# Asking for the expert weights batch by batch, each pair of transfers behind the turned attention weights of its batch

## The chip, the core and the metric

The kernel runs on one core of a Trainium2 chip. The core has engines that work side by side, each with a queue of its own that is worked off in order: TensorE (matrix products; PE in the profile, its weight loads PEld), VectorE (DVE), ScalarE (ACT), GpSimd (POOL) and SyncE (SP, which here only issues transfers). Sixteen transfer engines (DMA) move data between the main memory (HBM) and the core's memory (SBUF); they are fed by a hardware queue, filled from SyncE, and by a software queue, filled from GpSimd. The metric is the device time of one execution in microseconds (us), the median over runs.

## The reference

Two stages. The first is a Nyström attention over 8 batches and 8 heads, 576 positions, 64 values a head; the second sends each of the 4608 tokens through one of 8 experts.

```python
q_lm, k_lm = means of 18 neighbouring rows of q, k      # 32 landmarks a head
A  = softmax(q    @ k_lm.T)                             # 576 x 32
Bm = softmax(q_lm @ k_lm.T)                             # 32 x 32
C  = softmax(q_lm @ k.T)                                # 32 x 576
Z  = Bm.T / (norm1(Bm) * norminf(Bm) + 1e-6)
for _ in range(6): Z = 2 * Z - Z @ Bm @ Z               # inverse by iteration
x = A @ Z @ C @ v                                       # then tokens x 512

e_idx  = argmax(x @ w_gate); gate_w = softmax(x @ w_gate)[e_idx]
eom    = sigmoid(x @ w_output_gate)
out[i] = gate_w * eom[e_idx] * (relu(x[i] @ w1[e_idx]) @ w2[e_idx])
```

An expert has w1 of 512 x 1024 and w2 of 1024 x 512 in float32, 4 MB together, and 8 experts have 33.5 MB.

## The kernel before

The attention runs over the 8 batches, and in each over two halves of four heads; four heads of 32 landmarks fill the 128 partitions. The expert weights of all eight experts have a place of their own, the tile `wall`, which holds them as bfloat16; the transfer itself converts. `load_expert(e)` (L73 to L77) asks GpSimd's software queue for w1 (L74) and w2 (L76) of one expert. In the kernel before it is called at the head of batch `b` for expert `b` (L149). Nothing in the batch reads it.

For each half of a batch:

- SyncE asks for the v tile `vS` in three transfers (L156).
- `turned` (L112 to L132) is called for q and then for k. SyncE asks for the tile `nat` as it lies in memory (L116; two slots). VectorE turns it to `tr` (L118; three slots). GpSimd adds 18 rows to the landmark sums in five steps (L120 to L125, `t9` with one slot, result `lm`). VectorE turns `lm` to `lmT` (L127), and GpSimd builds the block-diagonal matrix `bd` from it (L130, twice, four slots).
- TensorE makes the landmark scores `pB` (L165), the scores of C and of A (both by the helper `scores`, L144), each from a `bd` and a `tr`.
- VectorE, ScalarE and GpSimd make the softmaxes. The last part of it, for A: VectorE turns the scores to `At` (L210) and takes the maximum `ax` (L212), GpSimd subtracts (L216), ScalarE exponentiates (L217), VectorE sums (L218), GpSimd multiplies (L220), and VectorE turns the result to `AT` (L222; four slots). `ATs[1]` is that of the second half.

After both halves, the inverse is iterated for both together (L230 on TensorE, L234 to L241 on VectorE, each step waiting for the one before), GpSimd spreads the result to `ZB` (L246), TensorE makes the gate logits `pL` (L267) and the rows `pX` (L276), ScalarE converts them to `xo` (L279), and SyncE stores them to `x_rows` in main memory (L280).

When all batches are done, the routing sorts the tokens by expert (L282 to L457). Then 43 tiles of 128 tokens go through the experts: GpSimd gathers rows of `x_rows` (L469), TensorE multiplies by the weights in `wall` (L488, L506) at an offset that is read from the sorted list, and GpSimd scatters the result (L511).

The order of each engine's queue is not written out by hand. A planner lays out all instructions when the kernel is built: it takes them in the order of the program as their priority, with its own model of when inputs and tile slots come free, and so mixes work of several batches. On the chip each queue then keeps that order. Semaphores are added so that an instruction waits for what it reads and overwrites; a waiting instruction holds up all behind it on its engine.

Of the kernel before, what the change touches and what calls it, by code (L numbers as in the profile page):

```python
# [36 lines left out]
def kernel(  # L37
# [11 lines left out]
    nc = tc.nc  # L49
# [12 lines left out]
    W1 = DCH * F  # L62
# [7 lines left out]
    gp = ctx.enter_context(tc.tile_pool(name="const", bufs=1))  # L70
    wall = gp.tile([128, E, WE], BF16)

    def load_expert(e):  # L73
        nc.gpsimd.dma_start(out=wall[:, e, :W1].rearrange("p (c f) -> p c f", f=F),  # L74
                            in_=moe_w1[e].rearrange("(c p) f -> p c f", p=128))
        nc.gpsimd.dma_start(out=wall[:, e, W1:].rearrange("p (c d) -> p c d", d=HD),  # L76
                            in_=moe_w2[e].rearrange("(c p) d -> p c d", p=128))  # L77
# [14 lines left out]
    with tc.tile_pool(name="attn_c", bufs=1) as cp, \  # L92
# [53 lines left out]
            return p[:, :, :NC]  # L146

        for b in range(B):
            load_expert(b)  # L149
            XW = sb.tile([128, 2, 128 + D], F32, tag="X", bufs=3)  # L150
            cc = sb.tile([128, 2], F32, tag="cc")
            ATs = []
            for hf in range(2):
# [67 lines left out]
                AT = sb.tile([128, S], F32, tag="AT", bufs=4)  # L221
                nc.vector.transpose(out=AT, in_=At.rearrange("p k r -> p (k r)"))  # L222
                ATs.append(AT)


            cur = XW
# [328 lines left out]
```

## Time and profile before

| | |
|---|---|
| median of 3 runs | 617.27 us (615.83 to 618.49) |
| the profiled execution | 616.98 us, its span 615.3 us |
| first and last start of a TensorE matmul on batch data | 27.5 us, 604.7 us |
| last `AT` turned | 327.1 us |
| last store to `x_rows` issued | 370.0 us |
| first gather of the experts' stage | 418.4 us |
| busy in the span | TensorE 465.4 us, GpSimd 286.6, VectorE 277.3, ScalarE 126.3 |
| weight transfers | 16, issued by GpSimd between 1.6 and 60.3 us |

A view of stages gives the busy microseconds of each engine in a stretch with the number of instructions in brackets, then the granted TensorE clock (1.00 is full speed), the mean busy share of the sixteen transfer engines, and the rate in GB/s. The share can exceed 1 where transfers overlap on an engine. A row of a timeline gives the start in us, the length in us, the engine and line, the operation with the tile written and the tiles read, the shape, the count, and in square brackets how long the engine had stood idle and what ended that. SPq marks the issue of a transfer on SyncE. A row of landing times gives the microseconds from the issue of a transfer to its end.

### The profile page before, as it was taken

The numbers are of one execution on the slowest core, as the hardware profiler recorded it, in microseconds if no ns is written. First come the engines' busy times: TensorE is split into PE (matmuls) and PEld (weight loads), VectorE is DVE, ScalarE is ACT, GpSimd is POOL, SyncE is SP. The second block draws the span as 40 slices with busy tenths as digits, with TensorE's granted clock in tenths as the row PEclk, the third lists the DMA queues.
The fourth block names the chain that finished last, engine by engine and source line by source line (L and its number), as shares of the span: only waits on it lengthen the run. The fifth ranks groups of instructions, "written<-read, shape, count | busy, mean of one in ns | idle before, by whom it ended". The sixth has DMA issues, their size and how long they took to land. (4 is left out here: it accounts for less than half of the span.)

```text
span 615.3 us, 9095 instructions
## 1 busy us (share of the span) xinstructions
PE 465.4 (76%) x3094; PEld 290.7 (47%) x3094; DVE 277.3 (45%) x681; ACT 126.3 (21%) x283; POOL 286.6 (47%) x408
## 2 busy tenths in 40 slices
PE   0231776788888788688798783494999999999993
PEld 0121453564666456365564442472555555555551
DVE  0223375374465546545462304991444444444442
ACT  0020121313232131222213120001222222222220
POOL 1754879628465574874712002005445445444321
PEclk9966597797798889898887776556999999999997
DMA  9999999552427053352310000002222222223200
GB/s 162 259 228 242 246 260 264 136 145 73 152 75 205 9 146 116 94 138 78 116 38 27 14 29 11 0 2 68 69 87 101 89 104 86 99 92 99 74 27 0
DMA packets 35948, 65.51 MB, mean 106 GB/s; under 512 B 5088, under 2 KB 24032, under 8 KB 35904
## 3 DMA queue, kind: packets, MB, share of 16 engines
q0 software_dynamic: 18048, 31.86, 22.9%
q1 hardware_dynamic: 17856, 33.07, 17.9%
q8 instruction: 27, 0.44, 0.3%
q14 instruction: 17, 0.14, 0.1%
HBM read 67.53 MB, written 15.99 MB: 136 GB/s over the span
## 5 line engine op out<-in xcount | busy, mean ns | idle before, releaser
L144 PE MATMUL p<-tr,bd 128*128 128x288 f32 x256 | 87.4, 465 | 44.9 <-POOL bd L130 44.1
L488 PE MATMUL ph<-wall,xT 128*128 x344 | 82.9, 385 | 2.3 <-issue 2.3
L511 POOL DMA_INDIRECT out_dram<-ysb,sca_i x43 | 43.5, 1012 | 81.9 <-DVE ysb L510 51.1
L506 PE MATMUL py<-wall,hT 128*128 x344 | 81.1, 379 | 0.0
L144 PEld LDWEIGHTS p<-tr,bd 128*128 128x128 f32 x256 | 51.8, 218 | 55.0 <-POOL bd L130 44.6
L492 ACT ACTIVATE h<-ph 128x512 bf16<-128x512 f32 x86 | 46.7, 594 | 138.4 <-PE ph L488 138.4
L469 POOL DMA_INDIRECT xs<-x_rows,gat_i x43 | 42.0, 976 | 65.7 <-DVE sca_i L456 42.6
L276 PE MATMUL pX<-ZB,AT 128*128 128x256 f32 (+1 forms) x160 | 54.8, 460 | 15.1 <-POOL ZB L246 7.6
L230 PE MATMUL pN<-nxt 128*128 128x192 f32 x192 | 46.6, 367 | 16.7 <-DVE nxt L238 11.9
L500 DVE COPY hT<-pht 128x1024 bf16<-128x1024 bf16 x43 | 29.7, 691 | 62.4 <-PE pht L498 62.4
L118 DVE STREAM_TRANSPOSE tr<-nat 128x1152 f32<-128x1152 f32 x32 | 43.5, 1360 | 25.6 <-DMA nat<-in_q_dram 20.8
L488 PEld LDWEIGHTS <-xT 128*128 128x128 bf16 x344 | 33.9, 99 | 43.9 <-issue 4.4
L120 POOL TENSOR_TENSOR t<-nat 128x576 f32<-128x576 f32 x32 | 44.9, 1404 | 15.7 <-DMA nat<-in_q_dram 14.9
L510 DVE TENSOR_SCALAR ysb<-py,coeff_s 128x512 f32<-128x512 f32 x43 | 32.3, 751 | 40.0 <-PE py L506 40.0
L230 PEld LDWEIGHTS pN<-nxt 128*128 128x128 f32 x192 | 35.0, 208 | 30.3 <-DVE nxt L238 20.3
L506 PEld LDWEIGHTS <-hT 128*128 128x128 bf16 x344 | 31.9, 98 | 30.7
L276 PEld LDWEIGHTS pX<-ZB,AT 128*128 128x128 f32 (+1 forms) x160 | 27.6, 198 | 30.7 <-ACT xo L279 11.3
L130 POOL TENSOR_TENSOR bd<-mask,lmT 128x128 f32<-128x128 f32 x64 | 27.8, 457 | 29.5 <-PE p L144 16.0
L216 POOL TENSOR_TENSOR At<-At,ax 128x576 f32<-128x576 f32 x16 | 18.5, 1157 | 42.3 <-DVE ax L212 42.2
L279 ACT CAST xo<-pX 128x512 bf16<-128x512 f32 (+1 forms) x40 | 23.4, 584 | 33.8 <-PE pX L276 28.5
L428 PE MATMUL pinv<-Vt,St 128*128 128x86 f32 x72 | 22.1, 465 | 8.7 <-DVE Vt L426 8.7
L498 PEld LDWEIGHTS <-h 128*128 128x128 bf16 x344 | 22.9, 98 | 11.1 <-ACT h L492 0.6
(143 smaller groups left out, 619.8 us busy)
## 6 DMA issues: line engine op xcount, KB each, us to landing
wall<-in_moe_w_dram POOLq DMA_DIRECT2D x16, 1024.0 KB, 32.5
vS<-in_v_dram SPq DMA_DIRECT2D x48, 192.0 KB, 3.8
nat<-in_q_dram SPq DMA_DIRECT2D x16, 576.0 KB, 5.3
nat<-in_k_dram SPq DMA_DIRECT2D x16, 576.0 KB, 5.0
x_rows<-xo SPq DMA_DIRECT2D x32, 128.0 KB, 1.7
xs<-x_rows,gat_i POOLq DMA_INDIRECT x43, 2.8
out_dram<-ysb,sca_i POOLq DMA_INDIRECT x43, 2.8
x_rows<-xo SPq DMA_DIRECT2D x8, 64.0 KB, 1.9
```

The source lines that it names most:

```text
L118: nc.vector.transpose(out=tr.rearrange("p k c r -> p (k c r)"), in_=nat.rearrange("p k d -> p (k d)"))
L120: nc.gpsimd.tensor_tensor(t9, nat[:, 0:9], nat[:, 9:18], op=ADD)
L144: nc.tensor.matmul(p[:, n, :NC], lhsT=bd[:, c].rearrange("p h r -> p (h r)"), rhs=rhs, start=(c == 0), stop=(c == 1))
L230: nc.tensor.matmul(pN[:, hf, :], lhsT=cur[:, hf, :128], rhs=cur[:, hf, :])
L276: nc.tensor.matmul(pX[:tk, hf * HH * D:(hf + 1) * HH * D], lhsT=ATs[hf][:, t0:t0 + tk], rhs=ZB[:, hf].rearrange("p h d -> p (h d)"))
L469: nc.gpsimd.indirect_dma_start(out=xs, out_offset=None, in_=x_rows, in_offset=bass.IndirectOffsetOnAxis(ap=gat_i[:, j:j + 1], axis=0))
L488: nc.tensor.matmul(ph[hf], lhsT=xT[:, dc, :], rhs=wf[:, bass.ds(we[j] + (dc * F + hf * 512), 512)], start=(dc == 0), stop=(dc == DCH - 1))
L492: nc.scalar.activation(out=hs[j][:, hf * 512:(hf + 1) * 512], in_=ph[hf], func=RELU)
L500: nc.vector.tensor_copy(hTs[j], pht)
L506: nc.tensor.matmul(py, lhsT=hT[:, fc, :], rhs=wf[:, bass.ds(we[j] + (W1 + fc * HD), HD)], start=(fc == 0), stop=(fc == FCH - 1))
L510: nc.vector.tensor_scalar(out=ysb, in0=py, scalar1=coeff_s[:, j:j + 1], scalar2=None, op0=MUL)
L511: nc.gpsimd.indirect_dma_start(out=out, out_offset=bass.IndirectOffsetOnAxis(ap=sca_i[:, j:j + 1], axis=0), in_=ysb, in_offset=None, bound ...
```

## The change

The call moves from the head of batch `b` to the point behind its second half, in front of the iteration. `load_expert` gets the tile `ATs[1]` as an argument. Before each pair of transfers GpSimd copies one element of that tile into the first element of the two places that the transfers will overwrite. The transfers overwrite what the copies wrote, so they cannot be issued before the copies, and these wait for the tile `AT` of the second half.

```diff
-    def load_expert(e):
+    def load_expert(e, after):
+
+        for c in (0, W1):
+            nc.gpsimd.tensor_copy(wall[:1, e, c:c + 1], after[:1, :1])
         nc.gpsimd.dma_start(out=wall[:, e, :W1].rearrange("p (c f) -> p c f", f=F),
                             in_=moe_w1[e].rearrange("(c p) f -> p c f", p=128))
         nc.gpsimd.dma_start(out=wall[:, e, W1:].rearrange("p (c d) -> p c d", d=HD),
                             in_=moe_w2[e].rearrange("(c p) d -> p c d", p=128))
@@
         for b in range(B):
-            load_expert(b)
             XW = sb.tile([128, 2, 128 + D], F32, tag="X", bufs=3)
@@
                 AT = sb.tile([128, S], F32, tag="AT", bufs=4)
                 nc.vector.transpose(out=AT, in_=At.rearrange("p k r -> p (k r)"))
                 ATs.append(AT)
+            load_expert(b, ATs[1])
 
 
             cur = XW
```

## Prediction

> **What bounds the kernel now.** I read the page first: how busy the engines and the transfer engines are along the span.
>
> ```profile
> span 615.3 us, 9095 instructions
> PE   0231776788888788688798783494999999999993
> DMA  9999999552427053352310000002222222223200
> q0 software_dynamic: 18048, 31.86, 22.9%
> ```
>
> The digits are tenths of a slice of 15.4 us. TensorE has almost nothing to do in the first four slices, while the transfer engines are full in the first seven. After that the roles turn over. The next view gives the stages, in its columns for stage, length, the five engines (PE, PEld, DVE, ACT, POOL), granted clock, transfer share and rate; the last row is from a second call of it.
>
> ```profile
> 0.00:27.50 27.50, 0.00 (x0) 0.00 (x0) 5.35 (x14) 0.00 (x0) 10.43 (x22) 1.00 1.00 211
> 27.50:61.00 33.50, 11.92 (x76) 8.43 (x76) 8.86 (x20) 4.12 (x8) 17.51 (x25) 0.66 1.17 233
> 61.00:101.00 40.00, 26.79 (x143) 18.50 (x143) 20.43 (x44) 5.58 (x13) 33.38 (x56) 0.80 1.15 256
> ...
> 139.00:324.00 185.00, 150.84 (x1125) 103.43 (x1125) 97.73 (x238) 47.88 (x121) 110.86 (x174) 0.89 0.36 103
> ...
> 418.40:615.30 196.90, 180.45 (x1204) 96.78 (x1204) 76.33 (x129) 46.67 (x86) 85.47 (x86) 0.96 0.24 78
> ```
>
> From 139 to 324 us TensorE is busy 150.84 of 185 us, 82%: it bounds that stage, with waits between. In the first 101 us it does 11.92 + 26.79 = 38.7 us of work, which at 82% would take 47 us. So 54 us of the start are lost to something else. What that is stands in SyncE's queue, in the landing times of the natural-order tiles `nat` (first those asked for before 15 us, then the one between 66 and 70 us, the one between 70 and 78, and all after 125 us) and in POOL's order of work.
>
> ```profile
> 5.45 0.44 SPq L116 DMA_DIRECT2D nat<-in_q_dram  x1
> ...
> DMA to landing us min/median/max: 13.0/14.2/15.5
> ...
> DMA to landing us min/median/max: 6.8/6.8/6.8
> ...
> DMA to landing us min/median/max: 6.1/6.1/6.1
> ...
> DMA to landing us min/median/max: 3.5/4.0/6.2
> ```
>
> ```profile
> 18.47 1.41 POOL L120 TENSOR_TENSOR t<-nat 128x576 f32<-128x576 f32 x1 [14.94 <-DMA nat<-in_q_dram]
> 19.82 0.80 POOL L74 DMA_DIRECT2D wall<-in_moe_w_dram  x1
> ...
> 27.01 0.86 POOL L130 TENSOR_TENSOR bd<-mask,lmT 128x128 f32<-128x128 f32 x2 [1.33 <-DVE lmT L127]
> 27.84 1.39 POOL L120 TENSOR_TENSOR t<-nat 128x576 f32<-128x576 f32 x1
> ...
> 37.05 0.92 POOL L76 DMA_DIRECT2D wall<-in_moe_w_dram  x1 [2.70 <-DMA wall<-in_moe_w_dram]
> 39.54 0.86 POOL L130 TENSOR_TENSOR bd<-mask,lmT 128x128 f32<-128x128 f32 x2 [1.58 <-DVE lmT L127]
> ...
> 60.30 0.92 POOL L76 DMA_DIRECT2D wall<-in_moe_w_dram  x1 [3.93 <-DMA wall<-in_moe_w_dram]
> 61.24 0.88 POOL L130 TENSOR_TENSOR bd<-mask,lmT 128x128 f32<-128x128 f32 x2
> ...
> 67.03 0.87 POOL L130 TENSOR_TENSOR bd<-mask,lmT 128x128 f32<-128x128 f32 x2
> ```
>
> The first q tile, asked for at 5.45 us, lands 13.0 us later; with no weights under way the median is 4.0. Then POOL, which adds up the landmarks and builds the block-diagonal `bd`, has the issues of the weight transfers among its additions and twice stands behind a weight transfer (2.70 and 3.93 us). The four `bd` of batch 0 (q and k of each half) are started at 27.01, 39.54, 61.24 and 67.03. TensorE waits for the first and the third:
>
> ```profile
> 61.76 2.29 PE L144 MATMUL p<-tr,bd 128*128 128x288 f32 x4 [12.72 <-POOL bd L130]
> ```
>
> **The change part by part.** The sixteen weight issues leave the head of POOL's queue. Their prices:
>
> ```profile
> L74 POOL DMA_DIRECT2D wall<-in_moe_w_dram x8: 787/792/977, 1.6 to 55.2; - x8
> L76 POOL DMA_DIRECT2D wall<-in_moe_w_dram x8: 914/917/961, 2.6 to 60.3; - x8
> ...
> L488 PE MATMUL ph<-wall,xT x344: 376/379/634, 423.7 to 598.6; 128*128 x172
> ...
> DMA to landing us min/median/max: 8.5/32.5/54.9
> ```
>
> *Step 1, first q tile.* It no longer shares the engines with a pair of weight transfers, but still with the v and k tiles. Bounds: 4.0 us (the quiet median) and 13.0. I take 6.7, an estimate between the 6.1 and the 6.8 that single tiles took while weights still ran, since here three v transfers stand ahead of it on the queue. Gain 6.3 us. It lands at about 12.1.
>
> *Step 2, POOL up to the first `bd`.* Between 18.47 and 27.01 stand five issues, three of L74 and two of L76: 3 x 0.79 + 2 x 0.92 = 4.2 us. Gain so far 10.5, first `bd` at 16.5.
>
> *Step 3, up to the second `bd`.* Between 27.84 and 39.54 stand two L74, three L76 and the wait of 2.70: 1.6 + 2.8 + 2.7 = 7.0 us. Gain so far 17.5.
>
> *Step 4, up to the third `bd`.* Two of each and the wait of 3.93: 1.6 + 1.8 + 3.9 = 7.4 us. Gain so far 24.9 in POOL's present order; the fourth `bd` follows the third as before. That is one end. The other: the planner that orders the queues no longer sees the loads and may put the additions of the second half ahead of the work that waits for VectorE. Then POOL is bound only by its own additions, 4.3 us a tile (27.01 - 18.47 less the 4.2 of issues), so four tiles after 12.1 us end at 29.3 instead of 67.03: gain 37.7. What is late next there is the slot of the transposed tile `tr` (three of them), freed by the scores. I take 30, between the two ends.
>
> *Step 5, the issues come back.* Each batch now has, behind its last turned tile `AT`, two one-element copies and the pair of issues on POOL. The rows for the wait, and for the pace of the batches:
>
> ```profile
> 83.47 1.16 POOL L220 TENSOR_TENSOR At<-At,ax 128x576 f32<-128x576 f32 x1
> ...
> 100.97 1.41 POOL L246 TENSOR_TENSOR ZB<-mask,nxt 128x256 f32<-128x256 f32 x2
> ...
> 109.94 1.16 POOL L220 TENSOR_TENSOR At<-At,ax 128x576 f32<-128x576 f32 x1
> ...
> 140.92 1.16 POOL L220 TENSOR_TENSOR At<-At,ax 128x576 f32<-128x576 f32 x1 [0.58 <-DVE ax L219]
> ...
> 325.90 1.16 POOL L220 TENSOR_TENSOR At<-At,ax 128x576 f32<-128x576 f32 x1 [0.58 <-DVE ax L219]
> ...
> 355.76 1.41 POOL L246 TENSOR_TENSOR ZB<-mask,nxt 128x256 f32<-128x256 f32 x2 [15.54 <-DVE nxt L241]
> ```
>
> ```profile
> L222 DVE STREAM_TRANSPOSE AT<-At x16: 759/778/779, 55.0 to 327.1; 128x576 f32<-128x576 f32 x16
> ```
>
> POOL's own L220 is the input of that transposition, so in the worst order POOL waits its 0.78 us right behind L220. No row shows a one-element copy on POOL; the nearest small ones bound it:
>
> ```profile
> 0.31 0.10 POOL L539 MEMSET const-float32-0.0<- 128x1 f32 x1 [0.31 <-issue]
> ...
> 24.63 0.34 POOL L125 TENSOR_TENSOR lm<-t 128x64 f32<-128x64 f32 x1
> ```
>
> I take 0.2 us each, nearer the single-column row. So a pair costs POOL 0.8 + 0.4 + 1.7 = 2.9 us; seven pairs with work behind them, 20 us. Queued behind them are the additions and `bd` of a later batch, for which TensorE waits. The cover is TensorE's own work: from 139 to 324 us it waited for `bd` once in five batches,
>
> ```profile
> PE p L144 <- POOL bd L130: 3.8, 1, 3.8
> ```
>
> so I take a fifth to a quarter, 5 us. The ends are 0 (the issues are only moved, so a further gain is excluded) and 20 (the cover is gone).
>
> *Step 6, sharing.* The software queue took 22.9% of 615.3 = 141 us of all sixteen engines; the experts' stage used 0.24 x 196.9 = 47 of that at most, so a pair of weights takes about 94 / 8 = 11.7 us. A batch every 37.0 us ((325.90 - 140.92) / 5) uses 0.36 x 37.0 = 13 us without weights, and 25 of 37 with them. The engines do not become the bound. A tile that meets a pair lands in 6.1 to 6.8 us instead of 4.0; I cost that at nothing, because the tiles are asked for ahead of use (two `nat`, three `tr`). Rival 3 is the case without that cover.
>
> *Step 7, the last pair.* It is issued after 327.1 + 0.8 us. With the longest landing, 54.9 us, all is there by 385, against a first use at 423.7; both ends move together. Cost 0. The Trainium skill, in "DMA: Bandwidth & Descriptors", section "Rules for kernel authors", advises the opposite of this change: issue a transfer early and wait for it late. Taken alone it would leave only step 5, 622 us. The 13.0 beside 4.0 us disagrees: early transfers that nobody awaits delayed awaited ones.
>
> Not counted: the granted clock of 0.66 between 27.5 and 61 us, which may rise if TensorE is fed sooner (11.92 us at 0.89 would be about 3 us less).
>
> **Sum.** The profiled execution took 616.98 us, 0.3 below the median of 617.27. 617.0 - 30 + 5 = 592 us.
>
> **The rivals.**
>
> 1. *All of the start is won and the issues stay hidden.* Against it speak the `tr` slots; for it, POOL's 60% load (110.86 of 185). 617 - 37.7 = 579 us.
>
> 2. *The early gain is given back.* The L220 of second halves stand at 83.47, 109.94, 140.92: 26.5 and 31.0 us apart, against 37.0 later. Batches 1 and 2 caught up because the tail of the batch before them came late; if they run at 37.0 at once, 10.5 + 6.0 = 16.5 of the 30 us go. Against it: ZB went from 100.97 with nothing to catch up. 617 - 30 + 16.5 + 5 = 608 us.
>
> 3. *Slower: late `nat` tiles at every batch.* POOL and VectorE start a batch's front with them. If two of the four loads of a batch meet the pair, and each lands up to 2.8 us later on the path (6.8 against 4.0), that is 5.6 us a batch, 39 over seven, against 30 won: 617 - 30 + 39 = 626 us. It decides from 30 / 7 = 4.3 us a batch. For it: the 6.1 and 6.8 us above, taken beside weights. Against: after the start TensorE hardly waits for the front.
>
> 4. *Issues stretched by VectorE.* The pairs now meet a VectorE that is 53% busy (97.73 of 185) instead of 26% (8.86 of 33.5). The longest issue in the rows is 0.98 against 0.79, so a small stretch is possible. Fourteen issues each held for one transposition of a turned tile, 0.78, is 11 us: 617 - 30 + 5 + 11 = 603 us. The Trainium skill, in "SBUF — State Buffer", section "SBUF: two separate sides", says that some VectorE operations lock GpSimd out while it writes descriptors; the rows of this trace, 787 to 977 ns, show little of it.
>
> **How the numbers follow.** Forecast (582 to 602) 0.56, rival 1 0.14, rival 2 0.14, rival 3 0.10, rival 4 0.06. The range 576 to 613 takes in rivals 1, 2 and 4; its upper end is 617 - 24.9 + 20, the smaller start gain with all of step 5 on the path. A measurement of this kernel tells from no change what is beyond about 0.5%, 3 us: faster 0.85, same 0.06 (rival 2 with a dear step 5, or a mild rival 3), slower 0.09.
>
> **What would show it.** Steps 1 to 4: first `nat` landing near 7 us after its issue, first TensorE matmul near 17 us, no L74 or L76 on POOL before 40 us, the first ZB near 70 us instead of 100.97. Step 5: the pairs right behind each second L220, with POOL idle for about 1 us there, and the ZB pace still near 36 us ((355.76 - 100.97) / 7 before). Step 6: `nat` landing in 4 to 7 us throughout. Step 7: no wait on `wall` at the first matmul of the experts. The prediction is wrong if the first ZB comes early but the pace grows to 40 us or more, or if POOL's order puts the copies ahead of additions that TensorE needs.

## The result, and the profile after

The changed kernel took 586.75 us (median of 4 runs, 582.71 to 590.14), the kernel before beside it 616.55; the ratio is 0.955, 95% interval 0.943 to 0.967. Forecast were 592 us with a range of 576 to 613. The profiled execution took 590.14 us, its span is 588.4, 26.9 less than before. Times are medians of all executions, ratios leave out the slow ones (over 1.5% above the fastest of the same kernel), and of two runs, all pairs behind batch 0 and the hold by the first half, only a slow execution was profiled, from which the order and the size of waits are read and nothing else. The page of the profile after:

```profile
span 588.4 us, 9095 instructions
...
PE   0656988769886697977788634948999999999993
...
DMA  6244945938794962876704500002322222233200
...
wall<-in_moe_w_dram POOLq DMA_DIRECT2D x16, 1024.0 KB, 10.4
```

TensorE now has work from the second slice on, and the transfers are spread over the attention instead of filling its first seven slices. A pair of weights lands in 10.4 us instead of 32.5. POOL's timeline, with the rows that answer to those shown of before (L120 is now L123, L130 is L133, L222 is L224 and L246 is L249; L76 is now the copy, and L77 and L79 are the pair):

```profile
12.76 1.39 POOL L123 TENSOR_TENSOR t<-nat 128x576 f32<-128x576 f32 x1 [11.26 <-DMA nat<-in_q_dram]
...
16.63 0.86 POOL L133 TENSOR_TENSOR bd<-mask,lmT 128x128 f32<-128x128 f32 x2 [0.36 <-DVE lmT L130]
...
21.34 0.86 POOL L133 TENSOR_TENSOR bd<-mask,lmT 128x128 f32<-128x128 f32 x2 [0.36 <-DVE lmT L130]
...
35.94 0.86 POOL L133 TENSOR_TENSOR bd<-mask,lmT 128x128 f32<-128x128 f32 x2
...
39.48 0.87 POOL L133 TENSOR_TENSOR bd<-mask,lmT 128x128 f32<-128x128 f32 x2 [0.36 <-DVE lmT L130]
...
56.86 0.31 POOL L76 CAST wall<-AT 1x1 bf16<-1x1 f32 x2
57.36 1.00 POOL L77 DMA_DIRECT2D wall<-in_moe_w_dram  x1 [0.20 <-POOL wall L76]
...
65.15 1.41 POOL L249 TENSOR_TENSOR ZB<-mask,nxt 128x256 f32<-128x256 f32 x2 [2.80 <-DVE nxt L244]
...
332.31 1.41 POOL L249 TENSOR_TENSOR ZB<-mask,nxt 128x256 f32<-128x256 f32 x2 [11.51 <-DVE nxt L244]
```

The four `bd` of batch 0 start 10.4, 18.2, 25.3 and 27.6 us earlier than before, and the first ZB 35.8 us earlier (65.15 against 100.97). The last ZB is only 23.5 us earlier (332.31 against 355.76). So 12.4 us were given back in between. Where they went is read from TensorE's busy time in the same stages of both kernels: up to the first ZB, then up to the seventh, then from the seventh to the end, then the whole attention. First before, then after, then the first two and the whole in a second profile of the same changed kernel:

```profile
0.00:100.97 100.97, 38.71 (x219) 26.93 (x219) 34.64 (x78) 9.70 (x21) 61.30 (x101) 0.81 1.11 236
100.97:323.91 222.94, 181.90 (x1350) 124.64 (x1350) 118.13 (x286) 57.31 (x143) 131.71 (x206) 0.88 0.41 113
323.91:372.37 48.46, 36.21 (x231) 20.68 (x231) 9.64 (x31) 11.05 (x29) 4.89 (x9) 0.75 0.08 25
0.00:372.37 372.37, 256.81 (x1800) 172.25 (x1800) 162.41 (x395) 78.07 (x193) 197.90 (x313) 0.84 0.55 135
```

```profile
0.00:65.15 65.15, 32.05 (x182) 22.39 (x183) 25.09 (x63) 6.97 (x15) 33.99 (x61) 0.82 0.48 126
65.15:306.68 241.53, 196.13 (x1389) 134.89 (x1387) 125.75 (x300) 59.09 (x149) 157.83 (x256) 0.86 0.68 160
306.68:346.30 39.62, 27.38 (x233) 16.54 (x232) 10.54 (x33) 11.50 (x29) 7.97 (x13) 0.99 0.42 84
0.00:346.30 346.30, 255.56 (x1800) 173.81 (x1800) 161.37 (x395) 77.55 (x193) 199.79 (x329) 0.87 0.61 145
```

```profile
0.00:60.90 60.90, 30.43 (x182) 21.02 (x183) 25.00 (x63) 6.96 (x15) 34.00 (x61) 0.80 0.52 135
60.90:298.37 237.47, 187.83 (x1389) 128.59 (x1387) 125.82 (x300) 58.99 (x149) 157.75 (x255) 0.90 0.69 163
0.00:338.00 338.00, 245.64 (x1800) 166.16 (x1800) 161.37 (x395) 77.44 (x193) 199.73 (x329) 0.89 0.63 148
```

Up to the first ZB TensorE stood idle 100.97 - 38.71 = 62.3 us before and 65.15 - 32.05 = 33.1 after: 29.2 us won. The other 6.7 of the 35.8 are matrix work that was done by then before and has still to be done after. From the first ZB to the end of the attention the idle time is 115.6 - 62.3 = 53.3 before and 90.7 - 33.1 = 57.6 after: 4.3 us lost. With 1.2 us less busy time this gives 26.1 us up to the start of the routing, and 0.8 come later. In the second profile 31.8 us of idle time are won, 8.6 are lost, and the busy time is 11.2 us less; so the loss is known only as 4 to 9 us, and the busy time moves between executions of one program. One part of the busy time differs in the same way in both profiles: from the seventh ZB on it is 27.4 us against 36.2 before, at a granted clock of 0.99 against 0.75. The loss of idle time has a row of its own in the view of waits after, which is not there before:

```profile
PE pX L279 <- ACT xo L282: 15.8, 18, 4.2
ACT xo L282 <- DMA x_rows<-xo: 13.5, 4, 5.0
```

Before, TensorE waited for `xo` like this:

```profile
PE pX L276 <- ACT xo L279: 7.4, 14, 0.7
```

ScalarE had to wait for a store of rows to land, four times and up to 5.0 us each, before it could fill that slot again; TensorE's wait for it went from 7.4 to 15.8 us.

### The profile page after: what moved, and what is told of

Its sections match the earlier page's. It is cut to its first block, busy times and chain, and to the rows that moved or that the text cites. A ratio compares the mean times of both kernels' runs of the same rounds, so it can differ in the third digit from the quotient of the medians.

```text
span 588.4 us, 9095 instructions
## 1 busy us (share of the span) xinstructions
PE 462.1 (79%) x3072; PEld 291.8 (50%) x3094; DVE 276.3 (47%) x681; ACT 125.8 (21%) x283; POOL 288.3 (49%) x424
## 5 line engine op out<-in xcount | busy, mean ns | idle before, releaser
L147 PE MATMUL p<-tr,bd 128*128 128x288 f32 x256 | 89.9, 476 | 28.0 <-DVE tr L121 18.0
L509 PE MATMUL py<-wall,hT 128*128 x323 | 76.7, 379 | 1.1
L147 PEld LDWEIGHTS p<-tr,bd 128*128 128x128 f32 x256 | 53.0, 224 | 38.7 <-POOL bd L133 29.3
L279 PE MATMUL pX<-ZB,AT 128*128 128x256 f32 (+1 forms) x160 | 52.1, 447 | 19.0 <-ACT xo L282 15.8
L503 DVE COPY hT<-pht 128x1024 bf16<-128x1024 bf16 x43 | 29.7, 692 | 62.5 <-PE pht L501 62.5
L123 POOL TENSOR_TENSOR t<-nat 128x576 f32<-128x576 f32 x32 | 44.9, 1403 | 14.1 <-DMA nat<-in_q_dram 11.3
L513 DVE TENSOR_SCALAR ysb<-py,coeff_s 128x512 f32<-128x512 f32 x43 | 32.3, 751 | 40.0 <-PE py L509 40.0
L121 DVE STREAM_TRANSPOSE tr<-nat 128x1152 f32<-128x1152 f32 x32 | 43.4, 1355 | 10.5 <-DMA nat<-in_q_dram 10.5
L282 ACT CAST xo<-pX 128x512 bf16<-128x512 f32 (+1 forms) x40 | 23.3, 583 | 46.0 <-PE pX L279 27.1
L133 POOL TENSOR_TENSOR bd<-mask,lmT 128x128 f32<-128x128 f32 x64 | 27.7, 456 | 7.3 <-DVE lmT L130 3.2
L241 DVE SCALAR_TENSOR_TENSOR nxt<-nxt,pN 128x384 f32<-128x384 f32 x40 | 21.5, 538 | 16.7 <-PE pN L233 16.5
## 6 DMA issues: line engine op xcount, KB each, us to landing
wall<-in_moe_w_dram POOLq DMA_DIRECT2D x16, 1024.0 KB, 10.4
```

The source lines that it names most:

```text
L121: nc.vector.transpose(out=tr.rearrange("p k c r -> p (k c r)"), in_=nat.rearrange("p k d -> p (k d)"))
L123: nc.gpsimd.tensor_tensor(t9, nat[:, 0:9], nat[:, 9:18], op=ADD)
L147: nc.tensor.matmul(p[:, n, :NC], lhsT=bd[:, c].rearrange("p h r -> p (h r)"), rhs=rhs, start=(c == 0), stop=(c == 1))
L279: nc.tensor.matmul(pX[:tk, hf * HH * D:(hf + 1) * HH * D], lhsT=ATs[hf][:, t0:t0 + tk], rhs=ZB[:, hf].rearrange("p h d -> p (h d)"))
L503: nc.vector.tensor_copy(hTs[j], pht)
L509: nc.tensor.matmul(py, lhsT=hT[:, fc, :], rhs=wf[:, bass.ds(we[j] + (W1 + fc * HD), HD)], start=(fc == 0), stop=(fc == FCH - 1))
```

## The experiments

Beside the first of these runs the changed kernel took 585.67 us and the kernel before 617.56; beside the later ones only the kernel before was measured again, at 615.1 to 617.0. Differences to the changed kernel are to the 585.67. Of the theories below, T says that the weight traffic itself is what the start lost, and I that the issues on POOL are. A says that the later loss is the price of the returned issues and of shared transfer engines, S that it is the stores of rows that the pairs slow down, and B that it is only early lead given back or a matter of the planner's order.

**The changed kernel again.**

> The changed kernel again, as the measure for the other runs beside it. Both theories: 583 to 590 us, first ZB near 65 us, last ZB 267 us later.

585.67 us (581.72 to 589.88). The profiled execution has its first ZB at 60.90 and the last 263.1 us later, against 65.15 and 267.2 in the first profile. The first q tile lands 5.2 us after its issue, against 7.5. The program is the same; the last section says what else differs.

**Place without hold.** Built without the two copies, with only the call moved, the queues of all five engines come out in the order of the kernel before. It is the copies that hold the transfers, not the place in the text: the planner lifts an issue that waits for nothing to the front. This was read from the built program and not run.

**Small transfers in the kernel before.**

```diff
+        if e < E - 1:
+            nc.gpsimd.dma_start(out=wall[:, e, :64], in_=moe_w1[e, :128, :64])
+            nc.gpsimd.dma_start(out=wall[:, e, W1:W1 + 64], in_=moe_w2[e, :128, :64])
+            return
```

> The kernel before with the pairs of experts 0 to 6 cut to 128 rows of 64 values (expert 7 whole and used by all tokens, the other experts left out); all sixteen issues stay at the head of POOL's queue. If the start is lost to traffic (landing of the first q tile 13.0 against 7.5 us, and POOL's waits of 2.70 and 3.93 behind weight transfers): first q tile lands near 7.5 us, first bd near 21, first ZB near 80 or below, total 590 to 600. If the start is lost to the issues themselves on POOL: first bd near 25, first ZB above 90, total 605 to 617.

588.05 us, ratio 0.954 (0.949 to 0.959): as fast as the changed kernel with nothing held, and below the 590 to 600 that was expected if traffic is the cause. POOL's timeline:

```profile
11.77 1.40 POOL L124 TENSOR_TENSOR t<-nat 128x576 f32<-128x576 f32 x1 [4.07 <-DMA nat<-in_q_dram]
...
18.23 0.87 POOL L134 TENSOR_TENSOR bd<-mask,lmT 128x128 f32<-128x128 f32 x2
...
60.75 1.41 POOL L250 TENSOR_TENSOR ZB<-mask,nxt 128x256 f32<-128x256 f32 x2 [1.07 <-DVE nxt L245]
```

That looks like theory T alone. But the planner put eleven of the sixteen issues ahead of the first addition, where POOL has nothing to do; so the run takes away both the traffic and most of the issues among the additions. The next two take them apart.

**Issues among the additions, without traffic.**

```diff
+        def small_issue(b, t9):
+            if b == 0:
+                ...
+                nc.gpsimd.tensor_copy(scr[:1, i, :1], t9[:1, 0, :1])
+                nc.gpsimd.dma_start(out=scr[:, i], in_=moe_w1[i % E, :128, :8])
...
             nc.gpsimd.tensor_tensor(t9, nat[:, 0:9], nat[:, 9:18], op=ADD)
+            small_issue(b, t9)
```

> The changed kernel, and in batch 0 sixteen further issues on POOL, one behind each of the first four additions of the four tiles, each held by a one-element copy of the sum before it; they carry 128 rows of 8 values to a scratch tile, so there are issues among the additions as in the kernel before, and almost no traffic. Theory I (the issues on POOL were a main part of what the start lost, 11.9 us by the prediction's steps 2 to 4): first bd 3 to 4 us later than in the changed kernel, fourth bd 12 to 16 us later, total 597 to 602. Theory T (the traffic was nearly all of it): the issues fall into POOL's idle time, fourth bd under 8 us later, total 586 to 592.

597.92 us (597.36 to 599.65): 12 us over the changed kernel, a total that theory I named. In POOL's timeline the first addition and the first and the fourth `bd`:

```profile
10.38 1.40 POOL L133 TENSOR_TENSOR t<-nat 128x576 f32<-128x576 f32 x1 [8.88 <-DMA nat<-in_q_dram]
...
18.06 0.87 POOL L147 TENSOR_TENSOR bd<-mask,lmT 128x128 f32<-128x128 f32 x2
...
47.43 0.87 POOL L147 TENSOR_TENSOR bd<-mask,lmT 128x128 f32<-128x128 f32 x2
```

From the first addition to the first `bd` it is 7.7 us against 3.9 in the changed kernel, to the fourth 37.1 against 26.7. Sixteen issues with their copies delay the fourth `bd` by 10.3 us (8.0 and 11.5 by the clock of the two profiles of the changed kernel, less than the 12 to 16 that theory I expected). But this delay is not what the 12 us at the end consist of. The first ZB stands at 67.31, 2.2 and 6.4 us later than in the two profiles, and the seventh follows it after 235.6 us, sooner than there (241.5 and 237.5). From the seventh to the end of the attention the run then takes 48.5 us instead of 39.6:

```profile
302.88:351.34 48.46, 36.28 (x231) 20.60 (x231) 9.65 (x31) 11.05 (x29) 6.92 (x13) 0.75 0.36 69
```

This is TensorE's busy time at a granted clock of 0.75 instead of 0.99, as in the kernel before, some 250 us behind the last of the sixteen issues. These 8.8 us are most of the 12, and no run shows that the issues cause them.

**Traffic without issues among the additions.** A first attempt used ScalarE's queue:

```diff
+        for e in range(E):
+            nc.scalar.dma_start(out=wall[:, e].bitcast(mybir.dt.uint16)..., in_=moe_w1[e].bitcast(mybir.dt.uint16)...)
```

> The changed kernel, and at its head eight further transfers of 2 MB each from ScalarE's queue into the places of the expert weights (raw 16-bit words of w1, overwritten later by the held pairs, so the result is the same): traffic at the start, and no issue more on POOL. Theory T: the first q tile lands 11 to 13 us after its issue, later tiles in 5 to 10 us, the first ZB is 12 to 25 us later than in the changed kernel, total 597 to 612. Theory I: the first ZB is under 8 us later, total 586 to 594.

610.33 us, inside theory T's range, but it does not show it. ScalarE itself stood behind its own issues:

```profile
0.80 43.30 ACTq L117 DMA_DIRECT2D wall<-in_moe_w_dram  x8
```

It could do no softmax until 44 us. The run with the same idea on POOL, at a time when POOL is idle anyway:

```diff
+        for e in range(0, E, 2):
+            nc.gpsimd.dma_start(out=wall[:, e]..., in_=moe_w1[e:e + 2]...)
+            nc.gpsimd.dma_start(out=wall[:, e + 1]..., in_=moe_w2[e:e + 2]...)
```

> The changed kernel, and at the head of POOL's queue eight further transfers, each of two experts' w1 or w2, into places that the held pairs overwrite later: the weight traffic of the kernel before, all asked for while POOL has nothing else to do, with ScalarE's queue free and no issue among the additions. It repairs the run with ScalarE's queue, where ScalarE itself stood until 44 us behind its own issues. Theory T (traffic alone is most of what the start lost): first q tile lands 11 us or more after its issue, first ZB 10 to 25 us later than in the changed kernel, total 597 to 610. Theory I (the issues and POOL's waits were most of it): first ZB under 8 us later, total under 596.

593.52 us (591.80 to 596.09), 8 us over the changed kernel: under theory I's bound of 596, although the first q tile lands 14.2 us after its issue, as theory T has it. The timeline:

```profile
19.93 1.41 POOL L129 TENSOR_TENSOR t<-nat 128x576 f32<-128x576 f32 x1 [9.98 <-DMA nat<-in_q_dram]
...
68.58 1.41 POOL L255 TENSOR_TENSOR ZB<-mask,nxt 128x256 f32<-128x256 f32 x2
```

The q tile, asked for at 5.62 us, starts POOL at 19.93, which is 7.2 and 9.4 us later than in the two profiles of the changed kernel (12.76 and 10.51). The first ZB is 3.4 and 7.7 us later. The late tile is not the only thing that this traffic delays: the eight transfers take up to 97 us to land, and ScalarE waits 27.7 us, nine times, for stores of rows, against 13.5, four times, in the changed kernel. So all the weight traffic of the kernel before, asked for at once, cost 8 us here, where no engine had to stand for it, and what these 8 us consist of was not taken apart.

**All pairs behind one batch.** Two places for eight pairs: behind batch 0, and behind batch 7.

```diff
-            load_expert(b, ATs[1])
+            if b == 0:                     # second run: b == B - 1
+                for e in range(E):
+                    load_expert(e, ATs[1])
```

> All eight pairs are held until the AT of batch 0 alone, and none later. If only the first batch matters: first ZB near 65, and from then the issues and the traffic hurt less than they did at the head, total 588 to 596. If keeping the pairs apart matters too (POOL stands behind earlier transfers where sixteen issues are in a row: a new one has to wait until one of the eight before it has landed): POOL waits of 25 to 50 us in front of the ZB of batch 0, total 600 to 620.

> All eight pairs are held until the AT of the last batch, so the attention runs with no weight traffic and no issues in it. Theory A (the 12.4 us by which the last ZB follows the first one later than before are the price of the returned issues and of shared transfer engines): first ZB near 64, last ZB 255 us after it, near 319, the rows stored near 334. Theory B (that loss is the early lead given back, or the planner's new order, whatever the loads do): last ZB again 267 us after the first, near 331. In both, the first weight of the experts comes late: eight pairs of 11.7 us from about 317 (B) or 305 (A) end near 411 or 399, against a first use near 397 or 385, so 14 us more there. Total: A 588, B 600.

642.21 us behind batch 0 (ratio 1.036, 1.029 to 1.043), slower than both kernels and than the 620 expected at most; 619.04 behind batch 7 (1.003, 1.001 to 1.006). POOL's timeline behind batch 0, from the eighth issue to ZB, and then, behind batch 7, who waited for `wall` and how long and how often:

```profile
63.43 0.97 POOL L79 DMA_DIRECT2D wall<-in_moe_w_dram  x1
66.20 0.76 POOL L77 DMA_DIRECT2D wall<-in_moe_w_dram  x1 [1.80 <-DMA wall<-in_moe_w_dram]
71.98 0.88 POOL L79 DMA_DIRECT2D wall<-in_moe_w_dram  x1 [5.02 <-DMA wall<-in_moe_w_dram]
...
102.03 0.88 POOL L79 DMA_DIRECT2D wall<-in_moe_w_dram  x1 [4.32 <-DMA wall<-in_moe_w_dram]
102.93 1.41 POOL L251 TENSOR_TENSOR ZB<-mask,nxt 128x256 f32<-128x256 f32 x2
```

```profile
POOL wall L77: 13.3, 3
POOL wall L79: 12.3, 3
```

Eight issues go out without a wait, and each of the other eight stands until an earlier transfer has landed, 32 us in all, with all of POOL's queue behind it, ZB included. The run behind batch 7 also answers theory A, since it has no weights in the first seven batches:

```profile
65.64 1.42 POOL L251 TENSOR_TENSOR ZB<-mask,nxt 128x256 f32<-128x256 f32 x2 [4.84 <-DVE nxt L246]
...
301.64 1.41 POOL L251 TENSOR_TENSOR ZB<-mask,nxt 128x256 f32<-128x256 f32 x2 [1.77 <-DVE nxt L246]
354.87 1.41 POOL L251 TENSOR_TENSOR ZB<-mask,nxt 128x256 f32<-128x256 f32 x2
```

First to seventh ZB took 236.0 us, against 241.5 and 237.5 in the two profiles of the changed kernel and 222.9 before. So most of the slower pace is there without any weights, as theory B has it. It is not there as idle time of TensorE, which is 42.4 us in this stretch (236.0 less 193.6 busy), against 45.4 and 49.6 in the changed kernel and 41.0 before; and ScalarE waits 0.7 us, once, for a store of rows before 305 us, but 12.3 us, four times, once the pairs are under way. As far as two orders can be compared, the idle time that was lost thus comes with the weights. Neither total was met: both expected the price at the first weight of the experts, and it fell on the last ZB, 53 us behind the seventh.

**Small transfers in the changed kernel.** The edit of the small transfers, on the changed kernel.

> The changed kernel with the pairs of experts 0 to 6 cut to 128 rows of 64 values (expert 7 is loaded whole, and all tokens use it, so the result leaves out the other experts); the copies, the waits and sixteen issues stay. If sharing of the transfer engines costs the 12.4 us of pace (theory A1): first to last ZB 255 us, total 575. If the returned issues and copies on POOL cost it (A2) or the lead is given back or the order is worse (B): first to last ZB 263 to 267, total 583 to 590.

591.36 us (588.12 to 599.14), not faster than the changed kernel and above both expected totals. ScalarE's wait for stores fell from 13.5 to 3.1 us,

```profile
ACT xo L286 <- DMA x_rows<-xo: 3.1, 1, 3.1
```

but the cheaper transfers also changed the planner's order in all queues. The run does not decide on the price of sharing.

**A third slot for the rows.** This leaves the planner's order nearly as it is. For the space, the tiles `ZT` and `ZV` go from two slots to one.

```diff
-                xo = sb.tile([128, HD], BF16, tag="xo")
+                xo = sb.tile([128, HD], BF16, tag="xo", bufs=3)
```

> The changed kernel with three slots for the converted rows xo instead of two (ZT and ZV go from two to one for the space); the orders of the queues stay nearly the same. In the changed kernel ScalarE waited 13.5 us in all, four times, for a store of rows to land before it could fill the slot again, and in the kernel before not at all. If that wait reaches the end (theory S: the pairs cost by slowing the stores): it falls under 5 us, total 576 to 582. If it lies beside other work: 584 to 590.

574.07 us (573.07 to 575.53), ratio 0.933 (0.926 to 0.940): 11.6 us under the changed kernel and the fastest version here. The waits:

```profile
PE pX L279 <- ACT xo L282: 9.7, 18, 0.7
...
ACT xo L282 <- DMA x_rows<-xo: 5.8, 2, 2.9
```

Both fell, by 6.1 and 7.7 us. TensorE's longest wait is 0.7 us again, as before the change. The wait for stores fell to 5.8, not under 5. The gain is larger than the waits, and not all of it is theirs: TensorE's idle time from the first ZB to the routing is 53.3 us, 4.4 and 8.6 less than in the two profiles of the changed kernel and as much as before the change. The rest of the 11.6 is busy time, which by itself differs by 10 us between those two profiles. Beside the second one, whose busy time in the attention is the same (245.6 us; 245.4 here), the span is 6.9 us shorter. The small differences of order were not taken out.

**Other tiles to hold by.** By the iterated inverse, right behind ZB, with two slots for `xo` and with three (and one for `ZT` and `ZV`); and by the `AT` of the first half.

```diff
-            load_expert(b, ATs[1])
+            load_expert(b, cur.rearrange("p a d -> p (a d)"))   # behind ZB
+            load_expert(b, ATs[0])                              # another run
```

> The pair of a batch is held by the iterated inverse instead of the turned attention weights, so it stands right behind ZB on POOL, which waits for the same tile. If POOL's wait for AT (0.5 to 1 us a batch) reaches the end: 3 to 6 us faster than the changed kernel, 580 to 583. If it is covered: 584 to 590, and what differs comes from the planner's order.

> The kernel that holds the pairs by the iterated inverse, with three slots for xo; the order of all five queues is the same as in it with two. There ScalarE waited 45.7 us, 15 times, for stores of rows. Theory S: the wait falls under 20 us and the total by 15 us or more, to 600 to 608. If the 36 us that this place costs over the changed kernel come from the planner's order: 615 to 625.

> The changed kernel with the pair held by the AT of the first half instead of the second, so that it goes out some 10 us earlier in each batch and has mostly landed before the batch's rows are stored. Theory S: ScalarE's wait for stores falls under 8 us, total 578 to 584. Otherwise 584 to 595, with the differences of a new order.

Behind ZB: 622.96 us with two slots (ratio 1.012, 1.006 to 1.019), where 580 to 590 was expected, and 614.77 with three, in the same order of all queues, nearer the 615 to 625 expected of the order than the 600 to 608 of theory S. ScalarE's wait for stores:

```profile
ACT xo L282 <- DMA x_rows<-xo: 45.7, 15, 5.4
```

```profile
ACT xo L282 <- DMA x_rows<-xo: 18.6, 9, 3.0
```

The rows of a batch are stored right behind its ZB, so here pair and stores meet in every batch. The third slot takes 27.1 us off the wait and 8.2 off the time, in an unchanged order; TensorE's idle time falls by 5.7 us. So the stores' delay reaches the end, at less than a third of its size. The two were measured beside different runs of the kernel before, which were 1.2 us apart. The other 29 us over the changed kernel are not explained by it: about 10 of them are idle time of TensorE, and the rest is mostly its busy time, at a granted clock of 0.77 in the last batch. Held by the first half: 607.16 us (0.985, 0.976 to 0.994), against an expectation of 578 to 584 or 584 to 595. ScalarE waits 35.7 us for stores there, eight times, where the expectation had under 8; the earlier pair does not get out of their way. Why these places are so much dearer stays open. The planner's order is other in each of them; it was not held fixed.

## Why the prediction was right, point by point

The sum, 30 us won at the start and 5 given back, answers to TensorE's idle time in the attention, which each profile gives as the length of a stretch less the busy time in it (all in us; the last column is the granted clock from the seventh ZB on):

| profile | idle up to the first ZB | idle from there to the routing | both | busy | clock at the end |
|---|---|---|---|---|---|
| kernel before | 62.3 | 53.3 | 115.6 | 256.8 | 0.75 |
| changed | 33.1 | 57.6 | 90.7 | 255.6 | 0.99 |
| changed, second profile | 30.5 | 61.9 | 92.4 | 245.6 | 0.99 |
| small transfers before | 29.7 | 56.3 | 86.0 | 253.2 | 0.75 |
| issues alone | 35.0 | 59.3 | 94.3 | 257.1 | 0.75 |
| traffic alone, on POOL | 36.8 | 58.4 | 95.2 | 250.2 | 0.98 |
| third slot for `xo` | 32.3 | 53.3 | 85.6 | 245.4 | 0.95 |
| behind ZB, two slots | 31.3 | 76.3 | 107.5 | 269.6 | 0.72 |
| behind ZB, three slots | 31.0 | 70.9 | 101.9 | 267.2 | 0.77 |

*The sum.* The idle time fell by 24.9 us in one profile and by 23.2 in the other; forecast were 25. The median fell by 29.8. The difference goes with TensorE's busy time, for which the prediction named the granted clock and counted nothing. It looked for a rise between 27.5 and 61 us; up to the first ZB the clock is 0.82 and 0.80, against 0.81 before. It rose in the last batch, which takes 8.8 us off the busy time, and between the first and the seventh ZB it lies on both sides of the 0.88 before (0.86 and 0.90). Executions of both kernels with the same mean granted clock are 23 to 24 us apart: 604.58 and 605.98 us at 0.889 and 0.887 before, 581.72 at 0.888 with the change. Why the last batch runs at another clock stays open.

*Step 1* (first q tile lands 6.7 us after its issue, 6.3 won): it lands in 7.5 us and in 5.2 in the second profile, and POOL starts 5.7 and 8.0 earlier. Right.

*Steps 2 and 3* (first `bd` at 16.5, second at 22.0): 16.63 and 21.34 (14.39 and 19.09 in the second profile). Right. For the issues alone steps 2 to 4 have 4.2 + 4.4 + 3.4 = 12 us, and the run with issues alone is 12 us slower. That these agree is luck: 8.8 of its 12 us are the clock of the last batch, and TensorE's idle time is only 2 to 4 us more. That the issues delay the `bd` is shown; that they are worth 12 us is not.

*Step 4* (25 to 38 us at the fourth `bd`, 30 taken): 27.6, and 31.1 in the second profile. The idle time of TensorE won up to the first ZB, 29.2 and 31.8 us, is near the same 30. That the weights at the head of the queue cost this much is shown twice, by the changed kernel and by the kernel before with small transfers. How it divides among traffic, issues and POOL's waits behind transfers (6.6 us, not measured alone) is not: traffic alone and issues alone add only 2 to 5 us each to TensorE's idle time, against the 23 to 25 between the kernels. That POOL's waits can be dear is shown by the 32 us of the run behind batch 0.

*Step 5* (5 us by issues, copies and the wait for AT): the loss of idle time behind the first ZB is 4.3 us, and 8.6 in the second profile. The size was about right and the reason wrong. The copies take 0.18 us each, POOL waits 0.2 us for its own copy before an issue, and the wait for AT adds up to 2.4 us:

```profile
L76 POOL CAST wall<-AT x16: 176/176/179, 56.9 to 316.7; 1x1 bf16<-1x1 f32 x16
...
DVE AT L224: 2.4, 3
```

But what stands in front of TensorE is *step 6*, costed at nothing. The prediction looked at the `nat` tiles, which are asked for ahead of use, and they did hold: they land in

```profile
DMA to landing us min/median/max: 3.7/4.8/10.5
```

for all asked for after 100 us: a median of 4.8 against 4.0 before, the longest 10.5. It left out the stores of rows, which share the same engines, have two slots and are waited for at once. Their delay was worth about 4 to 9 us: with the third slot the idle time behind the first ZB is what it was before the change, which leaves next to nothing for the issues and copies. The pace from the first to the last ZB grew from 36.4 us a batch to 38.2 and 37.6, still under the 40 that the prediction gave as a sign of being wrong.

*Step 7*: no wait on `wall` at the experts' first product. Right: the last pair is issued by 317.8 us, none takes longer than 16.9 us to land, and the first use is at 397.1.

*The rivals.* Rival 2, lead given back, happened in part: 6.7 us of work less was done by the first ZB, against the 16.5 us that it had. It did not cost time of its own, since work that is left over is no idle time. The prediction took its 30 from POOL's lead at the fourth `bd` and not from idle time; that the two came out alike it had not worked out. Rival 3's late `nat` tiles did not come: behind 100 us no engine waited for one. Rival 4's stretched issues did not either:

```profile
L77 POOL DMA_DIRECT2D wall<-in_moe_w_dram x8: 790/790/997, 57.4 to 317.1; - x8
L79 POOL DMA_DIRECT2D wall<-in_moe_w_dram x8: 899/909/960, 58.3 to 317.8; - x8
```

These medians are 0.79 and 0.91 us, no longer than before, beside a VectorE that is 52% busy (125.75 of 241.53 us). The trap that the Trainium skill names in "SBUF — State Buffer", section "SBUF: two separate sides", does not show here.

## What to carry to other kernels

A transfer that nobody awaits yet is not free: it delays awaited ones in the shared engines, and its issue takes 0.8 to 0.9 us of the queue it stands in; where that queue feeds the critical chain, this delays what stands behind it (the fourth `bd` by 10.3 us here). If transfers are moved, look for every tile that shares the engines, stores too, and count its slots: the tile with two slots and no lead is where sharing is paid (4 to 9 us of idle time here, bought back with a third slot). And a planner that builds the queues lifts an issue to where it is ready, so only a data dependence holds it, and each other place of that dependence gives another order; the two tried here came out 21 and 37 us slower than the first, for reasons that are in part open. Last, a total that agrees with a forecast term is no proof of it: look in which stretch the difference lies, and whether it is idle time or busy time.

## What the runs showed of the hardware

The same program gave two profiles with spans of 588.4 and 580.0 us. TensorE's instructions are the same (22 records are missing from the first), but took longer in the first, at mean granted clocks of 0.872 and 0.888; the lines of engines of the two pages:

```profile
PE 462.1 (79%) x3072; PEld 291.8 (50%) x3094; DVE 276.3 (47%) x681; ACT 125.8 (21%) x283; POOL 288.3 (49%) x424
```

```profile
PE 453.3 (78%) x3094; PEld 284.1 (49%) x3094; DVE 276.3 (48%) x681; ACT 125.7 (22%) x283; POOL 288.2 (50%) x424
```

VectorE, ScalarE and POOL agree within 0.1 us, and TensorE differs by 8.8 (by 9.9 in the attention, where no record is missing), about the whole difference of the spans. A difference of a few microseconds between two single profiles of such a kernel need therefore not be an effect of an edit. The second finding: the granted clock can differ in one stretch and not in the next. From the seventh ZB to the routing nearly the same 231 to 233 matmuls take 27.4 us of TensorE's time at 0.99 (changed kernel, both profiles) and 36.2 to 36.3 at 0.75 (kernel before, and the run with issues alone). No run shows what sets it. The third: in these programs eight weight transfers are under way at most; in the run behind batch 0 a ninth issue stands, and its engine with it, until an earlier one has landed, and from then on one goes out every 5 us.
